# A performer attention and token/channel mixer on one Trainium2 core: the order of all jobs, their buffer slots and the choice of eviction engines are made anew

## The chip, the cores and the metric

The kernel runs on one NeuronCore of one Trainium2 chip. TensorE (PE) multiplies matrices into PSUM banks; VectorE (DVE), ScalarE (ACT) and GpSimd (POOL) do the elementwise work and move results out of PSUM; SyncE (SP), ACT and POOL also issue DMAs. Each engine works through its own list of instructions in order and waits on semaphores for the others. The metric is device microseconds for one execution of the whole kernel, as the median of several runs.

## What is computed

The reference, cut to what matters: random-feature attention (a "performer") for 8 batches, 8 heads, 576 positions and head size 64 with 128 features, and behind it a mixer over tokens (256 hidden) and over channels (512 wide, 1536 hidden).

```python
def phi(x):
    proj = np.einsum('bhsd,md->bhsm', x, omega)
    sq = np.sum(x * x, axis=-1, keepdims=True) / 2.0
    h = proj - sq
    h = h - np.max(h, axis=-1, keepdims=True)
    return np.exp(h) / np.sqrt(m)
q_p, k_p = (phi(q_s), phi(k_s))          # q, k times 1 / 64 ** 0.25
kv = np.einsum('bhsm,bhsd->bhmd', k_p, v)
z = np.sum(k_p, axis=2)
num = np.einsum('bhsm,bhmd->bhsd', q_p, kv)
den = np.einsum('bhsm,bhm->bhs', q_p, z)[..., None] + 1e-06
x = (num / den)                          # heads side by side: (8, 576, 512)
h = np.maximum(xt @ w_tok1, 0.0) @ w_tok2   # xt: x with tokens last
u = x + h.transpose(0, 2, 1)
out = u + np.maximum(u @ w_ch1, 0.0) @ w_ch2
```

## The kernel before

Matmuls take f16 operands, and PSUM holds f32 in eight banks of 128 x 512. Work is cut into some 1200 numbered jobs: a matmul job fills one bank (four matmuls of 512 columns for a channel job `c1`), an eviction job empties it.

For each batch b from 0 to 7 there are these stages. k and q are loaded and turned so that the head dimension lies on the partitions (`kT`, `qT`): batches 0 and 1 on TensorE (`first_rows`, `rows`, evicted by `first_out` and `rows_out`), the later ones by a cast to a scratch in DRAM and a transposing DMA that SP issues (`back`, L380). Each batch has 576 positions; the last 64 of all heads go together as a tail (`kt`, `qt` and what belongs to them). `kp` and `qp` multiply by omega, and ACT evicts them with the exponential (`kp_exp`, `qp_exp`, helper line L515). DVE takes a maximum for k (`km`, L681), v is scaled by it (`vs_`, L689, by the helper `tt` at L295), `kv` sums over the positions, and its eviction is `kv_out` (kvsb). `num` multiplies by qp, and DVE divides on eviction (`num_out`, L744 and L745). The token mixer is `t1` with a relu, `t2` and `uadd`; `ut_dma` (L799) is SP's transposing DMA that makes `uT`, the channel mixer's input. Batch 0 makes it on TensorE instead (`ut_`, evicted by `ut_out`).

The channel mixer runs over nine blocks c: 512 positions of each batch, and c8 with the 64-position tails of all batches. `c1` (L967, for the first two jobs of c0 split into L973 and L975) has twelve jobs of 128 hidden rows by 512 positions, each with a `relu` to `r` (L290 on ACT, L292 on DVE). Block 0 multiplies by the second weight wc2 in the usual way (`c2`, L1001). The others use one level of Strassen's scheme (`channel_out_fast`): eight sums of halves of r for each block (L877, by `tt`), seven products (L917), and reads that add them up in the output tile (`read`, L906), then stores. The differences of wc2's quarters that it needs are four `T` jobs on DVE (L448), which need both halves of wc2 (L440).

The order is not found at build time. Three tables hold it. ORDER lists the job numbers; `Planner.run` (L137) goes through it and issues each job on its engine, so each engine's list of instructions is ORDER cut to its jobs. A negative number n is a warm-up: a matmul of zeros into bank -1-n (L1039), of which there are 23. SLOT gives each buffer of a ring (banks, kT, qT, uT, r and others) its place in the ring, in the order in which they are first taken. MOVED overrides the engine of a job by its number:

```python
def engine(self, usual):
    return MOVED.get(len(self.jobs), usual)
```

The helper of the elementwise sums looks at the name of the engine in this way, while evictions have a form for ACT and one for DVE:

```python
def tt(eng, **kw):
    (nc.gpsimd if eng == "POOL" else nc.vector).tensor_tensor(**kw)
```

In the old order SP issues a first k load (job 4, L385), omega (job 2, L395) and a second k load (6); ACT issues the other two k loads (3 and 5). Job 7 is the k tail's load, 0 the identity matrix, both on POOL. Job 39 is the transpose of omega (L452), 41 and 44 are `first_rows` (L470), 47, 48, 67 and 68 belong to the k tail of batch 0. POOL issues the loads of v, q, the weights and the casts, in one queue.

Of the kernel before, what the change touches and what calls it, by code (L numbers as in the profile page):

```python
# [81 lines left out]
]  # L82
SLOT = (
    "0001203450670100531642027046313724005203716031213170242506371243501030126450300623741115037622415010"
    "3157143302010163207240531170360711422336140014632220751302761220105427113005401216030201704522131743"
    "5632010231741610520432015370243105072320714330625120712006304015123156124230220105611334112101502001"
# [985 lines left out]
```

## Time and profile before

| | us |
|---|---|
| median of 3 runs | 282.96 (282.94 to 283.96) |
| span of the profiled execution, first to last instruction | 281.1 |
| TensorE busy in it | 270.3 |
| VectorE busy | 222.4 |
| ScalarE busy | 138.6 |
| GpSimd busy | 92.0 |

The profiled execution is known by its span; the runs' times contain what lies around it, so the median is 1.9 us above this span. In the profile "PE" is a matmul, "PEld" a load of weights. L967 is line 967 of the kernel as listed above. In rows of waits, "A <- B" means that A waited for B. In the changed kernel all lines behind the tables have a number lower by 18.

### The profile page before, as it was taken

Reading aid. Unit: us, or ns where it says so; the run is one execution under the profiler, and the core shown is the slowest. Engines: PE = TensorE matmul, PEld = TensorE weight load, DVE = VectorE, ACT = ScalarE, POOL = GpSimd, SP = SyncE. Lnnn points to the kernel's source line nnn. Section 1 sums busy time; section 2 is a strip of 40 time slices with the busy share of each in tenths; the row PEclk is TensorE's granted clock in tenths of the full one; section 3 lists DMA queues with packets and bytes.
Section 4 is the critical chain, followed back from the end, with each engine's and each line's share of the span. In section 5 each row is a group of like instructions: output and inputs, shape, how many; then the busy total and the mean of one; then the engine's idle time right before and its main releaser. Section 6 shows DMA issues by size and latency. Waiting matters only on the chain.

```text
span 281.1 us, 6278 instructions
## 1 busy us (share of the span) xinstructions
PE 270.3 (96%) x2526; PEld 167.6 (60%) x2526; DVE 222.4 (79%) x462; ACT 138.6 (49%) x288; POOL 92.0 (33%) x116
## 2 busy tenths in 40 slices
PE   6899999999999999999999999999999999999993
PEld 2547546443657755665667647755676467446782
DVE  2589828499999899996997999977995893565992
ACT  1498994049676418743758445734753510031200
POOL 8574994007510872048008710510033000000001
PEclk9999999999999999999999999999999999999999
DMA  6999999999998999997979993960151304030125
GB/s 161 194 189 161 157 169 213 178 191 202 179 218 184 148 172 186 181 198 104 212 178 185 241 135 101 161 156 2 76 97 59 111 0 96 0 149 2 75 90 135
DMA packets 80524, 39.66 MB, mean 141 GB/s; under 512 B 63984, under 2 KB 76016, under 8 KB 80304
## 3 DMA queue, kind: packets, MB, share of 16 engines
q0 software_dynamic: 31744, 17.74, 44.1%
q1 hardware_dynamic: 46832, 15.77, 29.1%
q10 hardware_dynamic: 1920, 5.77, 5.4%
q8 instruction: 19, 0.31, 0.4%
q14 instruction: 9, 0.07, 0.1%
HBM read 35.95 MB, written 16.52 MB: 187 GB/s over the span
## 4 chain that ended last, share of the span: by engine, by line
PE 89%; DVE 3%; DMA 2%; ACT 2%; issue 0%; SPq 0%; DVEq 0%
PE bank L967 32%; PE bank L917 26%; PE bank L791 5%; PE bank L778 5%; PE bank L1001 4%; PE bank L735 3%; PE bank L657 3%; PE bank L702 3%; DMA wc<-in_k_dram 2%; PE bank L669 2%; ACT kp L515 1%; PE bank L845 1%; PE bank L817 1%; PE bank L737 1%; PE bank L771 1%; DVE T L448 1%
## 5 line engine op out<-in xcount | busy, mean ns | idle before, releaser
L967 PE MATMUL bank<-uT,wc 128*128 128x512 f16 x376 | 89.6, 379 | 0.5 <-DVE r L292 0.4
L290 ACT ACTIVATE r<-bank 128x512 f16<-128x512 f32 (+1 forms) x86 | 47.7, 601 | 82.7 <-PE bank L967 61.5
L295 POOL TENSOR_TENSOR vs<-v,vs 128x512 f16<-128x512 f16 x32 | 34.2, 1072 | 94.4 <-DVE vs L683 51.3
L967 PEld LDWEIGHTS <-wc 128*128 128x128 f16 x424 | 38.8, 98 | 38.8 <-issue 1.6
L917 PEld LDWEIGHTS <-r 128*128 128x128 f16 x384 | 36.8, 98 | 8.2 <-issue 1.1
L515 ACT ACTIVATE kp<-bank 128x512 f16<-128x512 f32 x64 | 36.7, 618 | 8.9 <-PE bank L657 7.1
L515 ACT ACTIVATE qp<-bank 128x512 f16<-128x512 f32 x64 | 36.7, 614 | 8.8 <-PE bank L669 5.8
L681 DVE TENSOR_REDUCE km<-kp 128x8 f16<-128x1024 f16 x32 | 38.7, 1208 | 1.2 <-ACT kp L515 1.1
L292 DVE TENSOR_SCALAR r<-bank 128x512 f16<-128x512 f32 (+1 forms) x40 | 26.3, 670 | 15.7 <-PE bank L967 11.3
L745 DVE TENSOR_TENSOR x<-bank,rc 128x320 f16<-128x320 f32 x62 | 30.5, 492 | 2.1
L917 PEld LDWEIGHTS <-S 128*128 128x128 f16 x288 | 28.1, 98 | 5.8 <-issue 0.3
L906 DVE TENSOR_TENSOR o<-u,bank 128x512 f32<-128x512 f16 x28 | 19.0, 679 | 6.2 <-PE bank L917 5.8
L917 PE MATMUL bank<-T,r 128*128 128x256 f16 x192 | 23.8, 273 | 0.0
L917 PE MATMUL bank<-wc,r 128*128 128x256 f16 x192 | 23.6, 273 | 0.0
L917 PE MATMUL bank<-T,S 128*128 128x256 f16 x192 | 23.4, 273 | 0.0
L946 POOL DMA_DIRECT2D out_dram<-o x2 | 1.3, 645 | 61.2 <-issue 61.2
L906 DVE TENSOR_TENSOR o<-o,bank 128x512 f32<-128x512 f32 (+1 forms) x27 | 16.6, 617 | 2.5 <-PE bank L917 1.8
L735 PEld LDWEIGHTS <-qp 128*128 128x128 f16 x256 | 13.5, 98 | 8.1 <-DVE kvsb L286 0.7
L794 DVE TENSOR_TENSOR u<-x,bank 128x512 f16<-128x512 f16 x28 | 17.6, 680 | 0.0
L735 PE MATMUL bank<-kvsb,qp 128*128 128x65 f16 x256 | 15.0, 193 | 0.5 <-DVE kvsb L286 0.5
L791 PE MATMUL bank<-r,w 128*128 128x512 f16 x56 | 14.1, 381 | 0.0
L744 DVE RECIPROCAL rc<-bank 128x5 f32<-128x5 f32 x62 | 11.4, 184 | 2.9 <-PE bank L737 2.2
(119 smaller groups left out, 379.0 us busy)
## 6 DMA issues: line engine op xcount, KB each, us to landing
out_dram<-o ACTq DMA_DIRECT2D x9, 512.0 KB, 2.7
q<-in_q_dram POOLq DMA_DIRECT2D x6, 576.0 KB, 9.7
wc<-in_moe_w_ch_dram POOLq DMA_DIRECT2D x4, 768.0 KB, 9.0
k<-in_k_dram POOLq DMA_DIRECT2D x6, 512.0 KB, 7.8
v<-in_v_dram POOLq DMA_DIRECT2D x6, 512.0 KB, 9.9
out_dram<-o SPq DMA_DIRECT2D x5, 512.0 KB, 3.9
r<-in_q_dram POOLq DMA_DIRECT2D x4, 288.0 KB, 7.5
v<-in_v_dram POOLq DMA_DIRECT2D x4, 256.0 KB, 8.1
```

The costliest lines, as they stand in the source:

```text
L290: nc.scalar.activation(out=out, in_=in_, func=AF.Relu)
L292: nc.vector.tensor_relu(out=out, in_=in_)
L295: (nc.gpsimd if eng == "POOL" else nc.vector).tensor_tensor(**kw)
L515: nc.scalar.activation(out=out, in_=in_, func=AF.Exp, bias=0.0, scale=1.0)
L681: nc.vector.reduce_max(out=mx, in_=kpv, axis=AX.X)
L735: nc.tensor.matmul(ps[:, k, j * 65 : (j + 1) * 65], st, s[:, i, 0 : D + 1], start=True, stop=True)
L745: nc.vector.tensor_tensor(out=t_x[place("x", b)][:, :, (2 * hp + hs[0]) * D : (2 * hp + hs[0] + n) * D].rearrange("p j (i d) -> p i j d", ...
L791: nc.tensor.matmul(ps, w2_of(tb, j), r1[:, tb, :], start=(tb == 0), stop=(tb == NT - 1))
L794: nc.vector.tensor_tensor(out=t_u[place("u", b)][:, j, :], in0=t_x[place("x", b)][:, j, :], in1=bank(n), op=ALU.add)
L906: nc.vector.tensor_tensor(out=o, in0=a, in1=ps, op=ALU.add)
L917: nc.tensor.matmul(ps[:, j * DH : (j + 1) * DH], a[:, cb, j * P : (j + 1) * P], w[:, cb, :], start=(bank_of(b, j0) not in held and j == j0 ...
L967: nc.tensor.matmul(ps, wc1[:, db, cb * P : (cb + 1) * P], moving(db), start=(db == 0), stop=(db == ND - 1))
```

## The change

All three tables are replaced; everything below them is the same. The diff, cut to its core:

```diff
 ORDER = [
-    4, 3, 0, 2, 5, 7, 1, 6, 16, 14, 10, 15, 9, 8, 12, 38, 11, -1, -2, -3, -4, -5, -6, -7, -8, 39, 41, 13, 44,
-    42, 21, 40, 47, 45, 48, 76, 22, 46, 77, 67, 43, 68, -4, -6, 120, 18, 105, 78, 107, 82, -3, 49, 71, 106, 122,
-    -5, 90, 51, 111, 91, -4, -4, 52, 17, 70, 19, 121, 50, 53, 83, 54, 92, 126, -5, -5, -5, -1, -1, -6, -3, -1,
-    72, 69, 30, 108, 79, 110, 84, 112, 80, 96, 55, 81, 127, 113, 74, 73, 123, 109, 75, 28, 128, 124, 85, 114,
-    86, 57, 56, 97, 115, 88, 129, 87, 125, -8, 61, 20, 93, 89, 98, 94, 23, 116, 130, 134, 95, 131, 31, 99, 117,
...
+3, 7, 2, -1, 5, 4, 0, -2, 6, 10, 1, 9, 8, 12, 38, 39, 11, 40, 16, 13, 47, 48, 21, 67, -3, 68, 22, 41, 70, -3, 42, 43, -6, 14, 69, 76, 90, 18, 78, -2,
+91, 17, -3, 44, 77, 71, -6, 92, 49, 82, -6, 45, 50, 105, 52, 96, 107, 19, 79, 106, -6, 83, 46, -6, -2, 53, 81, 120, 30, 84, 51, 121, 108, 122, 54, 97,
+-1, 109, 93, 111, -6, 94, 72, 28, 74, 55, 110, 98, 85, 112, 95, 57, -8, -2, 73, 123, 126, 56, 219, 75, 80, 61, 20, 99, -3, 221, 63, -5, 88, 125, 127,
+100, -5, 89, 220, 86, 113, 101, 23, 87, 247, 114, 102, 103, -1, 31, 104, 134, 124, 115, 62, 24, 117, 128, 249, 118, 116, 64, 25, 135, -4, 129, 119,
+65, 205, 460, 130, 138, 131, 248, 132, 142, 66, 207, 58, 196, 139, 133, 236, 29, 60, 140, 143, 206, 59, 146, 33, 141, 253, 202, 238, 197, 144, 199,
...
+331, 161, 213, 327, 167, 256, 229, 214, 259, 332, 257, 230, 231, 241, 171, 164, 242, 152, 258, 215, 217, 165, 191, 34, 243, 260, 176, 216, 245, 181,
+244, 232, 186, 246, 182, 218, -8, 35, 261, -8, 264, 36, 262, 329, 265, 183, 263, 177, 184, 268, 328, 266, 269, 272, 267, 270, 178, 273, 271, 187, 179,
...
 ]
 SLOT = (
-    "0001203450670100531642027046313724005203716031213170242506371243501030126450300623741115037622415010"
...
+    "01010100340320541102600152431270053104716020340560417031361152065020430205006217105233076430123006145037007216470265210413670057622436061720"
...
 )
 MOVED = {
-    42: "DVE", 43: "ACT", 45: "ACT", 48: "DVE", 51: "ACT", 53: "ACT", 56: "ACT", 60: "ACT", 62: "ACT", 65:
-    "ACT", 75: "DVE", 129: "ACT", 137: "DVE", 139: "DVE", 141: "DVE", 145: "ACT", 147: "DVE", 163: "ACT", 169:
-    "DVE", 171: "ACT", 175: "DVE", 179: "ACT", 190: "ACT", 194: "ACT", 228: "ACT", 242: "DVE", 256: "DVE", 265:
-    "DVE", 278: "DVE", 280: "DVE", 286: "DVE", 300: "DVE", 324: "ACT", 399: "DVE", 426: "DVE", 428: "DVE", 432:
-    "DVE", 434: "DVE", 484: "DVE", 498: "DVE", 552: "DVE", 556: "DVE", 562: "DVE", 593: "ACT", 594: "ACT", 634:
-    "DVE", 662: "DVE", 690: "DVE", 692: "DVE", 700: "DVE", 702: "DVE", 727: "ACT", 768: "DVE", 796: "DVE", 822:
-    "DVE", 828: "DVE", 830: "DVE", 836: "DVE", 838: "DVE", 863: "ACT", 904: "DVE", 970: "DVE", 997: "ACT", 998:
-    "ACT", 1024: "DVE", 1052: "DVE", 1088: "DVE", 1092: "DVE", 1094: "DVE", 1096: "DVE", 1098: "DVE", 1102:
-    "DVE", 1104: "DVE", 1108: "DVE", 1133: "ACT", 1134: "ACT", 1140: "DVE", 1148: "DVE", 1150: "DVE", 1152:
-    "DVE", 1160: "DVE", 1200: "SP", 1205: "ACT", 1206: "SP", 1207: "ACT", 1208: "SP",
+42: "DVE", 43: "ACT", 45: "ACT", 46: "ACT", 50: "ACT", 56: "ACT", 60: "ACT", 114: "ACT", 129: "ACT", 143: "DVE", 147: "DVE", 163: "ACT", 175: "DVE",
+179: "ACT", 184: "ACT", 189: "ACT", 190: "ACT", 194: "ACT", 195: "ACT", 226: "DVE", 240: "DVE", 256: "DVE", 286: "DVE", 292: "DVE", 296: "DVE", 300:
+"DVE", 301: "ACT", 302: "ACT", 304: "ACT", 306: "ACT", 307: "ACT", 308: "ACT", 350: "DVE", 364: "DVE", 378: "DVE", 390: "DVE", 401: "DVE", 416: "DVE",
+422: "DVE", 424: "DVE", 428: "DVE", 436: "ACT", 440: "ACT", 441: "ACT", 526: "DVE", 568: "DVE", 570: "DVE", 571: "ACT", 573: "ACT", 574: "ACT", 576:
+"ACT", 577: "ACT", 578: "ACT", 620: "DVE", 648: "DVE", 671: "DVE", 692: "DVE", 696: "DVE", 702: "DVE", 704: "DVE", 706: "ACT", 707: "ACT", 708: "ACT",
+710: "ACT", 711: "ACT", 768: "DVE", 782: "DVE", 794: "DVE", 805: "DVE", 830: "DVE", 832: "DVE", 834: "DVE", 836: "DVE", 841: "ACT", 842: "ACT", 844:
+"ACT", 846: "ACT", 847: "ACT", 863: "ACT", 864: "ACT", 890: "DVE", 902: "DVE", 904: "DVE", 930: "DVE", 939: "DVE", 952: "DVE", 964: "DVE", 972: "DVE",
+977: "ACT", 978: "ACT", 980: "ACT", 981: "ACT", 982: "ACT", 998: "ACT", 1024: "DVE", 1038: "DVE", 1052: "DVE", 1066: "DVE", 1075: "DVE", 1088: "DVE",
+1090: "DVE", 1092: "DVE", 1096: "DVE", 1100: "DVE", 1104: "DVE", 1110: "DVE", 1111: "ACT", 1113: "ACT", 1114: "ACT", 1115: "ACT", 1116: "ACT", 1117:
+"ACT", 1134: "ACT", 1140: "DVE", 1144: "DVE", 1150: "DVE", 1154: "DVE", 1158: "DVE", 1163: "ACT", 1164: "ACT", 1166: "ACT", 1168: "ACT", 1169: "ACT",
+1170: "ACT", 1202: "ACT", 1205: "ACT", 1207: "ACT", 1208: "SP",
 }
```

What it changes, as read off the two orders:

- SP issues omega (2) ahead of its two k loads (4, 6). On POOL the load of the k tail (7) comes ahead of the identity matrix (0).
- Two warm-ups, in place of eight, stand ahead of the transpose of omega (39); the others lie between the first matmul jobs. The k tail of batch 0 (47, 48, 67, 68) comes before `first_rows` (41, 44).
- POOL's loads and casts keep their order. On SP some transposing DMAs and stores change places.
- The number of jobs of each kind stays. Six `vs_` products go from POOL to DVE; one copy `qt_dup` goes from DVE to POOL; DVE has 18 `kv_out` in place of 14, 42 channel and token relus in place of 40, 9 of 12 `rows_out` in place of 6; ACT has all four `out_copy` in place of two. Of the last stores ACT issues 7, SP 4 and POOL 1, where it was 4, 6 and 2.
- 42 of the 64 sums of Strassen's scheme are named "ACT" in MOVED.
- The first `T` (34) stands ahead of `num_out` jobs of batch 1 (260, 216, 244, 232, 246, 218). The `kt` matmuls of batch 4 stand some 20 us of TensorE work earlier.
- kT of batches 2 to 5 all take place 0 of their ring, those of 6 and 7 place 1; uT of all batches takes place 1. Banks are taken again at other distances.

More of the change, by code (lines that the diff above doesn't have):

```diff
@@ L22 @@
 ORDER = [
[59 rows of a table removed]
[42 rows of a table added]
 ]
 SLOT = (
-    "0001203450670100531642027046313724005203716031213170242506371243501030126450300623741115037622415010"
-    "3157143302010163207240531170360711422336140014632220751302761220105427113005401216030201704522131743"
-    "5632010231741610520432015370243105072320714330625120712006304015123156124230220105611334112101502001"
-    "1163320402165140211610176412517304000612037524002145223000117023104325137202120117305042100576141135"
-    "2740507154076110042751603114022705011041315732121403000112045010725110200405061403012301765403706427"
@@ L89 @@
-    "5643015206241073100625101246023220116534201330523111135160224716051246514725364700113516422103135174"
-    "1625317524300060120373642501100433627516043075122761076423700560420017305611117230017341570146002140"
-    "73521450047113602"
+    "01010100340320541102600152431270053104716020340560417031361152065020430205006217105233076430123006145037007216470265210413670057622436061720"
+    "10217061023450367235110020051716701522430123531704603214016201713715624011213064052173543104713226012702342011635004115012703116373160321053"
@@ L92 @@
+    "00312020061022012041141060701106270214133562047130201350362053206714313114070261702415310126716105113041510020123356012714201532411071260733"
+    "40734205370611400004131114105614261150172301702526420103215020506710417112616514302173236412460412700511510140301032741112063010422011322115"
+    "61502403717410023027170510651724336205303561070211406243206112107210142070406103622362411017472476167401470160162101411207270520257600702601"
+    "52110555006502415"
 )
 MOVED = {
-    42: "DVE", 43: "ACT", 45: "ACT", 48: "DVE", 51: "ACT", 53: "ACT", 56: "ACT", 60: "ACT", 62: "ACT", 65:
```

89 rows, old and new, of the table ORDER are left out of this document.

## The prediction

> **What bounds the kernel now.** I read the page from the top: the busy shares, the slices, and the chain that ended last.
>
> ```profile
> PE 270.3 (96%) x2526; PEld 167.6 (60%) x2526; DVE 222.4 (79%) x462; ACT 138.6 (49%) x288; POOL 92.0 (33%) x116
> PE   6899999999999999999999999999999999999993
> ACT  1498994049676418743758445734753510031200
> PE 89%; DVE 3%; DMA 2%; ACT 2%; issue 0%; SPq 0%; DVEq 0%
> ```
>
> TensorE is 96% busy and is 89% of the chain. The change keeps all 2526 matmuls, so it can only give back time in which TensorE has nothing to do. The windows show where that is, and ACT beside it: it is 49% busy over the run but 80 to 90% busy in slices 3 to 6 of 7 us each, 14 to 42 us.
>
> ```profile
> 0.00:10.00 10.00, 5.93 (x41) 3.08 (x42) 2.37 (x14) 1.28 (x1) 6.60 (x15) 1.00 0.87 168
> 10.00:20.00 10.00, 9.65 (x140) 5.00 (x137) 8.47 (x14) 8.84 (x20) 7.84 (x10) 1.00 1.22 205
> 20.00:33.50 13.50, 12.65 (x224) 9.23 (x224) 11.85 (x30) 12.59 (x35) 9.47 (x13) 1.00 1.04 149
> 33.50:276.10 242.60, 241.89 (x2128) 150.30 (x2127) 199.33 (x405) 115.90 (x234) 68.08 (x80) 1.00 0.76 137
> 276.10:281.10 5.00, 0.13 (x2) 0.00 (x0) 0.42 (x1) 0.00 (x0) 0.00 (x0) 0.89 0.54 146
> ```
>
> The columns after the length are PE, PEld, DVE, ACT, POOL (count in brackets), granted clock, DMA share and GB/s. From 33.5 us on TensorE is busy 241.89 of 242.60 us. The view of TensorE's waits over that stretch names only these two:
>
> ```profile
> PE bank L967 <- DVE r L292: 0.4, 1, 0.4
> PE bank L771 <- DVE x L745: 0.3, 1, 0.3
> ```
>
> Before 33.5 us the busy share misleads, since a recorded matmul is much longer than its turn. The chain has four L967 matmuls of 512 columns in 0.86 us, 0.215 each; at such paces the 405 matmuls before 33.5 us hold 16.0 us of real work and 4.9 us of warm-ups (23 x 0.215). Some 17.5 us without real work lie there. The chain of waits says on what:
>
> ```profile
> 0.74 0.68 SPq L385
> 1.48 0.57 SPq L395
> 2.09 6.97 DMA wc<-in_k_dram
> 9.10 1.12 PE bank L470 x13
> 13.32 1.57 ACT kp L515 x3
> 20.62 0.83 DVE qpt L631
> ...
> 32.80 0.70 DVE uT L286
> 33.54 1.02 PE bank L967 x4
> 41.07 0.86 PE bank L967 x4
> ```
>
> First the k loads (omega queued behind one on SP), then ACT's exponentials at 0.52 us each, then vector work up to the transposed mixer input uT, which frees the first channel matmul L967 at 33.54 us. Everything later is nearly gapless: what the change can win is that date, and the end.
>
> **The start.** SP now issues omega first: 0.74 us instead of 1.48. The POOL queue issues the k tails ahead of the identity matrix. TensorE does the k tails before the k rows, so ACT's first eviction no longer waits for the last k load.
>
> ```profile
> 6.40 0.29 PE L452 MATMUL bank<-ident,S 128*128 128x128 f16 x1 [1.61 <-DVE S L450]
> 10.16 0.59 ACT L286 CAST kT<-bank 128x512 f16<-128x512 f32 x1 [6.51 <-PE bank L470]
> L515 ACT ACTIVATE kp<-bank 128x512 f16<-128x512 f32 x13 | 7.8, 631 | 1.1 <-PE bank L657 1.0
> L515 ACT ACTIVATE qp<-bank 128x512 f16<-128x512 f32 x10 | 5.9, 643 | 0.5 <-PE bank L669 0.5
> ```
>
> (The last two rows are the groups of ACT from 10 to 33.5 us.) With omega 0.74 us sooner its transpose L452 runs at about 5.7 and ACT can start at about 7.0 in place of 10.16. The k load that SP moves back behind omega loses 0.74 us itself, but its rows are used later. Before the first L967 the old order holds 20.6 us of ACT work (each kind at its spacing when back to back, 0.52 for a kp): 10.16 + 20.6 + 1.6 idle = 32.4, and then DVE's km and uT end at 33.5. The new order has 22.35: more kp, qp, first_out and one more uT, less rows_out. Never idle, ACT ends at 7.0 + 22.35 = 29.35; with 1.0 of idle, 30.35; with uT evicted by ACT last and DVE's km no longer ahead of it the first L967 comes between 30.4 and 32.5 (if half of it fails). I take 31.0: 2.5 us earlier, and 0.3 us more real work is done by then (16.3 against 16.0).
>
> **What meets the earlier start.** The POOL order of the loads is kept, and they do not all come 2.5 us earlier.
>
> ```profile
> L440 POOL DMA_DIRECT2D wc<-in_moe_w_ch_dram x2: 846/862/877, 31.9 to 34.4; - x2
> DMA to landing us min/median/max: 7.4/10.3/12.7
> 47.68 4.10 PE bank L1001 x19
> 53.71 2.71 SPq L380 DMA_TRANSPOSE kT<-k  x1
> 60.55 1.85 SPq L799 DMA_TRANSPOSE uT<-u  x1
> 65.42 1.73 DVE T L448
> 67.92 1.89 PE bank L967 x8
> ```
>
> The last half of wc2 is issued at 34.4 and lands 12.7 later, at 47.1; L1001, its first reader, starts at 47.68. Ahead of it the queue ran at 149 GB/s from 20 to 33.5 us against 205 from 10 to 20. Were all that made up, (205-149)/205 x 13.5 = 3.7 us would come back; two dips, at 20 to 24 and 28 to 32 us, look like POOL issuing late, so I take 2.4. wc2 then lands at 44.7, and L1001, which comes at 28.9 us of real work in place of 29.2, can start at 44.8. The loads of k for batch 2 follow in the same queue, then kT's transpose (53.7) and uT's (60.55): about 2.4 earlier too. L967 of batch 1 starts near 63.05 instead of 64.95, but at 0.45 us less work done: 1.5 us of the gain is left at 65 us. Bounds: 0 (the queue saturated) and 2.5.
>
> **Engines and order afterwards.** Six vs products leave POOL for DVE, one dup copy (0.83 above) goes from DVE to POOL, and a few evictions change engine.
>
> ```profile
> L295 POOL TENSOR_TENSOR vs<-v,vs 128x512 f16<-128x512 f16 x32 | 34.2, 1072 | 94.4 <-DVE vs L683 51.3
> L295 DVE TENSOR_TENSOR S<-r 128x768 f16<-128x768 f16 x16 | 8.8, 551 | 0.6 <-ACT r L290 0.4
> ```
>
> No vs on DVE is in the trace; between the larger sum there, 0.551, and POOL's 1.072 I take 0.55: 3.3 us more on DVE over 200 us in which it idles 43, so nothing on the path (up to 6.4 us of DVE time, covered the same way; without the idle time it would delay evictions, rival 4). The T subtractions L448 that held L967 at 67.92 go ahead of num_outs as soon as wc2 is there, and the wait at L771 has another order: I take both waits, 0.4 + 0.3 = 0.7, as gone (bounds 0 and 0.7).
>
> The new order uses the PSUM banks more tightly. Counted over both orders after the start, a bank is taken again within 1.2 us of TensorE work after the job that filled it in 19 places before and 73 now, in 36 of these at about one job of four matmuls, 0.86.
>
> ```profile
> L967 PE MATMUL bank<-uT,wc 128*128 128x512 f16 x376 | 89.6, 379 | 0.5 <-DVE r L292 0.4
> L290 ACT ACTIVATE r<-bank 128x512 f16<-128x512 f32 (+1 forms) x86 | 47.7, 601 | 82.7 <-PE bank L967 61.5
> L292 DVE TENSOR_SCALAR r<-bank 128x512 f16<-128x512 f32 (+1 forms) x40 | 26.3, 670 | 15.7 <-PE bank L967 11.3
> ```
>
> A last matmul of 0.379 and an eviction of 0.601 or 0.670 free the bank 0.77 to 0.83 us after that matmul's turn of 0.215: inside 0.86, by 0.03 to 0.09 us, if the evicting engine is free. Where it isn't, TensorE stands. The small gaps of the old order at its 19 places come to about 0.8 us, an estimate from starts of neighbouring matmuls; scaled by 73/19, 2.3 us more. Bounds 0 and 2.3; I take 0.4, since in most of the 54 new places the engine has nothing queued by the order.
>
> The transposed loads have less room. The kt matmuls of batch 4 move some 20 us of work earlier and keep their kT buffer in one slot with the batch before; uT of batches 3 and 7 has 7.4 us between the last t2 matmul and the first L967, where it had 9.3 and 10.9.
>
> ```profile
> DMA to landing us min/median/max: 5.7/6.8/8.9
> ```
>
> This is kT's transpose from issue to landing: at its maximum 2.1 us over its median. I take nothing, as by my count the dates are just met; one late by half that, 1 us, at each of the three places costs 3 us.
>
> **The end.** The tail's stores lie differently: ACT issues seven, SP four, POOL one.
>
> ```profile
> 274.74 3.33 ACTq L946 DMA_DIRECT2D out_dram<-o  x4
> ```
>
> ACT's last four issues took 3.33 us; with one more at that rate behind the last read the end is up to 0.8 later; I take 0.2, since the last two issues are split over both queues as before.
>
> **The sum.** Start 1.5 + waits 0.7 - banks 0.4 - tail 0.2 = 1.6 us saved. The span of 281.1 becomes 279.5. The median of the runs lies 1.9 over the span (282.96 - 281.1), so the time is 281.4 us.
>
> **A rule against it.** The new order has 2 warm-ups ahead of the omega transpose, the old one 8:
>
> ```profile
> 1.19 3.60 PE L1039 MATMUL bank<-S 128*128 128x512 f16 x8 [1.19 <-DVE S L1036]
> 11.28 1.04 PE L1039 MATMUL bank<-S 128*128 128x512 f16 x2
> ```
>
> Eight in 3.60 us are 0.45 each, twice the 0.215 of later: TensorE starts at half pace although the granted clock reads 1.00, and two at 11.28 still take 0.52 each. The Trainium skill, "TensorE: Matmul & The Clock Gate", "Part 1: The HAM clock gate", says that the array starts at half clock and comes to full only after a busy window of about 3.4 us. The trace agrees with the first half; the eight did not hold the pace through the pauses behind them. By that rule the new order stays at half pace for longer, and it is a rival below.
>
> **The rivals.**
> 1. The whole start gain survives: POOL, no longer waiting, fills both dips and more, and wc2 lands as early as TensorE gets there. For it: DMA ran at 205 GB/s right before. Against it: each dip is only some 2 us deep, and more than 205 GB/s is in none of the windows. 1.0 to 1.3 more than in the sum: 280.2 us.
> 2. The queue holds all of it: wc2 lands at 47.1 as before, and L1001 and all after stand where they stood. 281.4 + 1.5 = 282.9.
> 3. Fewer warm-ups: if the real matmuls before 15 us, about 5 us of work, run at half pace, 5 us are added, but ACT's evictions bound that stretch, so 0 to 1.5 reach the first L967. With 1.0: 282.4.
> 4. Slower: banks. In all 54 new places evictions come 0.1 us later than planned (an ACT relu behind another eviction, a DVE one behind a 1.2 us km). The place is every L967 stretch from 65 us on; the price 54 x 0.1 = 5.4 in place of 0.4: 286.4. It decides where the last matmul's start to the end of the eviction exceeds 0.86 + 0.215 = 1.08 us, 0.1 over what the two rows add up to. For it: the margin is 0.03 to 0.09. Against it: the old order's 19 places cost about 0.04 each.
> 5. Slower: late transposes. kT of batch 4 and uT of batches 3 and 7 miss by about 1 us each: 284.4. For it: latencies spread by 2 us. Against it: a delay once taken moves all that follows, and the next has more room.
> 6. The change does not do what it says: it names ACT for 42 of the 64 Strassen sums (L295), but the helper for them knows only POOL and VectorE, so they stay on DVE. If the order counts on a free DVE there, the last sums of each of 8 blocks come some 0.6 late: 281.4 + 4.8 = 286.2. Against it: the sums stand in the order as close to the next DVE job as the ones named for DVE do.
>
> **How the numbers follow.** The forecast has 0.36, rival 1 0.15, 2 0.10, 3 0.05, 4 0.20, 5 0.10, 6 0.04. By its bounds the forecast's own case goes from 280.3 to 282.3. About 0.5%, 1.4 us, is what a measurement can tell here: faster means below 281.55, slower above 284.37. The forecast gives 0.27 to faster and 0.09 to no change; with rival 1 faster is 0.42. No change is 0.09 + 0.10 + 0.04 = 0.23. Rivals 4, 5, 6 and a rest of 3 make 0.35 slower. The range leaves out the best tenth (start gain 3 and both waits, 279.3) and the worst (above 286.8, half a us over rival 4): 279.3 to 286.8.
>
> **What would show it.** Right: L452 near 5.7 us, ACT's first eviction near 7, the first L967 near 31, L1001 near 44.8, L967 of batch 1 near 63, no wait at T, and the last 240 us gapless. Wrong: L1001 still near 47.6 (rival 2), warm-ups and kp matmuls at 0.4 past 12 us with a first L967 past 32 (3), many short gaps before L967 with ACT or DVE evictions as releasers (4), waits on kT or uT (5), S matmuls that wait for L295 (6).

## The result, and the profile after

The changed kernel takes 296.45 us (median) against 283.37 for the kernel before on the same chip: ratio 1.0441, interval 1.0381 to 1.0501. Timed again on another chip it is 1.0412 (1.0363 to 1.0461), 297.1 against 285.37. It is slower by about 12 us, where 1.6 us less was forecast. (One of its four first executions, the one profiled first, took 304.78 us; its extra 8 us are a single wait, told at the end. The profile below is of a later execution, e17, without that wait and with a span of 295.3 us. It lies 14.2 us above the trace of before, but the two come from different chips; timed side by side on the chip of e17 the difference is 11.7 us.)

The changed kernel: busy times, the slices of TensorE, and the windows that were shown of before.

```profile
PE 273.9 (93%) x2526; PEld 167.5 (57%) x2526; DVE 229.3 (78%) x471; ACT 138.4 (47%) x284; POOL 86.1 (29%) x110
...
PE   2999999999799799999969999999999999999991
```

```profile
0.00:10.00 10.00, 4.75 (x34) 1.93 (x36) 2.63 (x12) 3.27 (x7) 6.58 (x15) 1.00 0.89 170
10.00:20.00 10.00, 9.53 (x147) 4.96 (x145) 7.44 (x14) 9.35 (x20) 8.13 (x11) 1.00 1.22 205
20.00:33.50 13.50, 13.33 (x227) 9.46 (x226) 11.07 (x27) 12.61 (x34) 11.46 (x15) 1.00 1.20 175
33.50:276.10 242.60, 233.95 (x2021) 140.77 (x2020) 197.01 (x396) 113.13 (x225) 59.24 (x69) 1.00 0.75 130
```

In this execution the start is where it was: taken as one window, the first 33.5 us hold 400 matmuls, as against 398 (the sums over shorter windows, 408 and 405, count a matmul on an edge twice). The loss lies behind it. In the same stretch of 242.6 us TensorE does 2021 matmuls instead of 2128, and its busy time falls from 241.89 to 233.95. The other engines are busy for less of the stretch too, since less of the work passes in it: DVE 197.01 (199.33 before), ACT 113.13 (115.90), POOL 59.24 (68.08). Over the whole execution DVE has more to do, 229.3 us instead of 222.4, but that is 78% of a longer span. So TensorE waits on engines that are not full. These are the rows of 0.5 us and more behind the start in the view of its waits, where before only two rows stood in all:

```profile
PE bank L949 <- DVE o L888: 1.6, 1, 1.6
PE bank L651 <- DMA qT<-q: 1.5, 1, 1.5
PE bank L684 <- DVE u L776: 1.4, 1, 1.4
PE bank L773 <- DVE ut L833: 1.1, 1, 1.1
PE bank L899 <- DVE o L888: 0.9, 2, 0.6
PE bank L639 <- DVE r L274: 0.6, 1, 0.6
PE bank L773 <- DVE r L274: 0.5, 2, 0.3
PE bank L773 <- DVE u L776: 0.5, 1, 0.5
```

Seven of the eight wait for VectorE: for reads (`o`), adds of the token mixer (`u`, `ut`) and relus (`r`). With the smaller rows TensorE's waits for VectorE behind the start are 7.5 us, against 0.7 before. From the start of the first channel matmul to the start of the last matmul it takes 255.5 us, against 242.4: 13.1 us more. A count of work says in what pieces: it takes off each matmul's usual spacing from the next one's start, and what is left over is a gap. The gaps behind the first channel job are 17.0 us against 3.9 before by this count: some 31 of them are over 0.12 us and make 14.5 us (before 6, 1.6 us). The gaps below 0.12 us are 2.45 us in all against 2.29.

The largest shows how one comes about. TensorE and then DVE of the changed kernel around 97 us (start, duration, engine and line, and in brackets what ended an idle time):

```profile
96.96 0.41 PE L684 MATMUL bank<-vs,kp 128*128 128x65 f16 x8
97.20 0.22 PE L691 MATMUL bank<-vbd,kpt 128*128 128x130 f16 x1
99.03 1.24 PE L949 MATMUL bank<-uT,wc 128*128 128x512 f16 x5 [1.61 <-DVE o L888]
```

```profile
95.17 1.22 DVE L663 TENSOR_REDUCE km<-kp 128x8 f16<-128x1024 f16 x1
96.42 0.21 DVE L665 RECIPROCAL vs<-km 128x8 f16<-128x8 f16 x1
96.54 1.83 DVE L277 TENSOR_TENSOR S<-r,S 128x768 f16<-128x768 f16 x2
98.30 0.68 DVE L888 TENSOR_TENSOR o<-u,bank 128x512 f32<-128x512 f16 x1
```

L949 needs the bank that the read L888 empties. DVE gets to that read at 98.30, after two Strassen sums that take 1.83 us. Both are the last sums of block 1, and both are named "ACT" in the new table. The first takes 0.51 us, but the second 1.41, and it runs beside a product on POOL:

```profile
96.71 1.25 POOL L277 TENSOR_TENSOR vs<-v,vs 128x512 f16<-128x512 f16 x1 [0.39 <-DVE vs L665]
```

In the kernel before all 64 sums take 0.55 to 0.56 us, and none of them runs beside a POOL addition or product. Here four take 1.14 to 1.41. So of the 1.83 us that hold up the read, some 0.85 are that one of the sums is slow there.

### The profile page after: what moved, and what is told of

It reads as the page before. It is cut to its first block, busy times and chain, and to the rows that moved or that the text cites. A ratio compares the mean times of both kernels' runs of the same rounds, so it can differ in the third digit from the quotient of the medians.

```text
span 302.9 us, 6263 instructions
## 1 busy us (share of the span) xinstructions
PE 275.6 (91%) x2526; PEld 167.7 (55%) x2526; DVE 228.1 (75%) x471; ACT 138.2 (46%) x284; POOL 86.1 (28%) x110
## 4 chain that ended last, share of the span: by engine, by line
PE 62%; DVE 19%; DMA 10%; ACT 4%; issue 3%; SPq 1%; DVEq 0%; POOLq 0%
PE bank L949 19%; PE bank L899 19%; DMA kT<-k 8%; DVE S L277 4%; PE bank L760 4%; DVE x L727 3%; PE bank L773 3%; PE bank L983 3%; DVE r L274 3%; PE bank L639 2%; DVE o L888 2%; PE bank L651 2%; DVE km L663 2%; DMA r<-in_k_dram 2%; PE bank L684 2%
## 5 line engine op out<-in xcount | busy, mean ns | idle before, releaser
L949 PE MATMUL bank<-uT,wc 128*128 128x512 f16 x376 | 90.1, 379 | 1.6 <-DVE o L888 1.4
L949 PEld LDWEIGHTS <-wc 128*128 128x128 f16 x424 | 38.8, 98 | 42.7 <-issue 4.1
L277 POOL TENSOR_TENSOR vs<-v,vs 128x512 f16<-128x512 f16 x26 | 28.2, 1089 | 82.5 <-DVE vs L665 65.8
L274 DVE TENSOR_SCALAR r<-bank 128x512 f16<-128x512 f32 (+1 forms) x42 | 27.7, 667 | 21.9 <-PE bank L949 11.9
L497 ACT ACTIVATE qp<-bank 128x512 f16<-128x512 f32 x64 | 37.4, 615 | 4.9 <-PE bank L651 4.8
L888 DVE TENSOR_TENSOR o<-u,bank 128x512 f32<-128x512 f16 x28 | 19.1, 682 | 6.8 <-PE bank L899 6.7
L277 POOL TENSOR_TENSOR vbd<-vt,vbd 128x512 f16<-128x512 f16 x6 | 6.3, 1050 | 55.8 <-DVE vbd L576 28.4
L717 PEld LDWEIGHTS <-qp 128*128 128x128 f16 x256 | 14.2, 98 | 7.6 <-DVE kvsb L268 0.3
L888 DVE TENSOR_TENSOR o<-o,bank 128x512 f32<-128x512 f32 (+1 forms) x27 | 16.4, 621 | 2.5 <-PE bank L899 1.5
L717 PE MATMUL bank<-kvsb,qp 128*128 128x65 f16 x256 | 16.2, 193 | 0.0
L773 PE MATMUL bank<-r,w 128*128 128x512 f16 x56 | 14.8, 381 | 1.1 <-DVE u L776 0.5
## 6 DMA issues: line engine op xcount, KB each, us to landing
wc<-in_moe_w_ch_dram POOLq DMA_DIRECT2D x4, 768.0 KB, 10.9
```

The source lines that it names most:

```text
L274: nc.vector.tensor_relu(out=out, in_=in_)
L497: nc.scalar.activation(out=out, in_=in_, func=AF.Exp, bias=0.0, scale=1.0)
L717: nc.tensor.matmul(ps[:, k, j * 65 : (j + 1) * 65], st, s[:, i, 0 : D + 1], start=True, stop=True)
L773: nc.tensor.matmul(ps, w2_of(tb, j), r1[:, tb, :], start=(tb == 0), stop=(tb == NT - 1))
L888: nc.vector.tensor_tensor(out=o, in0=a, in1=ps, op=ALU.add)
L949: nc.tensor.matmul(ps, wc1[:, db, cb * P : (cb + 1) * P], moving(db), start=(db == 0), stop=(db == ND - 1))
```

## The experiments

**1. The same kernel again (e1), and one transposing load moved (e3).** The profile taken first had TensorE wait 7.8 us for the transposing load of k for batch 6 (job 869), which the new order issues ahead of two stores (458, 457).

> The changed kernel as it is, for a second profile; the first had the granted clock at 0.50 to 0.87 around 150 us and a TensorE wait of 7.8 us on the transposing load of k for batch 6. Theory A (that one load is the main loss): the wait is there again, 5 to 8 us, in a span near 294.5. Theory B (many small waits: tighter banks and fewer ring places): the wait at batch 6 is under 2 us, and 10 us or more are lost in pieces below 1.5 us.

```diff
 ORDER = [
...
-    455, 648, 452, 869, 446,
+    455, 648, 452, 446,
...
-    561, 548, 457, 664, 635,
+    561, 548, 457, 869, 664, 635,
```

> The changed kernel with the transposing load of k for batch 6 put back behind the two stores of block 2 in SP's queue, as before. If three transposing loads in a row beside v and q loads make it slow (A): it takes about 4 us instead of 17 to issue, TensorE waits for it at most 4 us, and the time falls by 4 to 8 us from a run with that wait. If the loss is many small waits (B): the time stays near 296.

e1: span 295.9 and 297.68 us, with no wait at batch 6; e3: span 295.4 and 297.77 us. Theory A falls for the loss as a rule: the 12 us are there without that wait. What e3 does in an execution that has it was not seen.

**2. omega ahead of k alone (e2).**

```diff
-    4, 3, 0, 2, 5, 7, 1, 6,
+    2, 4, 3, 0, 5, 7, 1, 6,
```

> The kernel before with one edit: SP issues omega ahead of its first k load. If the start hangs on omega: the first L967 up to 0.7 us earlier, 0.3 to 0.7 us less in all. If on the last k load or on ACT: within 0.3 us of before. Neither theory of the loss expects it slower by more than 0.5 us.

Ratio 0.9989 (0.9969 to 1.0009): nothing that can be told from no change. By the count of work the first channel job came 0.15 us earlier.

**3. Rings in turn (e4).** The new tables use place 0 of kT four times running, and place 1 of uT seven times. Here kT, qT, u, r1 and uT take their three places in turn, which changes 25 digits of SLOT:

```diff
 SLOT = (
-    "0101010034032054110260015243127005310471602034056041703136115206502043020500621710523307...
+    "0101010034032054110260015243127005310471602034056141703136115206502043020500621711523307...
```

> The changed kernel with the rings of kT, qT, u, r1 and uT used in turn over their three places, order and engines as in the changed kernel. If places taken again too soon hold up loads and writes (B, the rings): 3 to 8 us faster than the changed kernel, waits on kT, qT and u gone. If the rings do not matter: within 1 us of the changed kernel.

Ratio 1.0444 (1.0385 to 1.0502), and 12.5 us lost behind the start, as in e1. The places of these five rings do not matter.

**4. The sums that are named for ACT (e5, e6, and timed again as e18, e19 beside e17).** The labels change no instruction, but an order made in the belief that ACT does this work would give DVE's time to others. e5 lets ACT do as much as a sum would: a copy.

```diff
     def tt(eng, **kw):
+        if eng == "ACT":
+            return nc.scalar.copy(out=kw["out"], in_=kw["in0"])
         (nc.gpsimd if eng == "POOL" else nc.vector).tensor_tensor(**kw)
```

> The changed kernel, in which the 42 Strassen sums that are named for ACT are ACT copies of their first operand, so 42 additions are left out. If the order counts on ACT for them, and DVE has them on top (the rival of the prediction): TensorE's waits on DVE reads and uadds near 98, 150 and 153 us vanish, and the time falls by 4 to 9 us. If DVE's load there is not the cause: it falls by less than 2 us, or rises as ACT gets the work.

e6 leaves them on DVE, but short:

```diff
-                    tt(e_sum, out=o[:, part], in0=a[:, part], in1=b[:, part], op=op)
+                    w = slice(0, 32 if e_sum == "ACT" and c > 1 else 2 * P)
+                    tt(e_sum, out=o[:, part, w], in0=a[:, part, w], in1=b[:, part, w], op=op)
```

> The changed kernel, in which those of the 42 sums that belong to blocks 2 to 8 (36) stay on DVE but only add the first 32 of 256 columns of each piece; the rest is left out. DVE loses some 36 x 0.4 = 14 us of work and ACT gets none. If DVE's load is the cause: 4 to 9 us faster, as with the copies or more. If not: within 2 us of the changed kernel.

The first times were few and far apart (e5 287.98 and 292.24 us, ratio 1.0232, interval 1.0053 to 1.0412; e6 289.81 and 299.97 us), so both were timed again beside the changed kernel.

> The changed kernel again, timed beside the next two on one chip. By all theories 296 to 298.

> The 42 sums named for ACT as copies on ACT again (additions left out), timed in more rounds. If DVE's extra load is the larger part: 7 to 9 us below the changed kernel, so 288 to 290, and 4 to 6 over before.

> 36 of the sums cut on DVE again, timed in more rounds. If DVE's extra load is the larger part: 6 to 9 us below the changed kernel, 288 to 291. If the first times (289.8 and 300.0) meant that it does not help in general: above 293.

On that chip: changed 1.0412 (above), copies 1.0140 (1.0052 to 1.0228), cut 1.0156 (1.0092 to 1.0220). The cut takes 0.0256 x 285.37 = 7.3 us off the loss, the copies 7.8 by these ratios. The cut is the firm one: its four executions took 288.79 to 291.25 us, against 297.01 to 298.48 for the changed kernel. Those of the copies took 288.23, 291.08, 295.65 and 301.39; the ratio is of the two shortest, and the median of all four, 293.36, misses what was expected. The one of 295.65 left a trace: there TensorE waits 5.1 us for transposing loads of q and k, and 0.6 us for VectorE.

The traces say the same with less scatter. TensorE's waits for VectorE behind the start, 7.5 us in the changed kernel (7.3 in e1), are 0.4 with copies (e5) and 2.8 with cut sums (e6, e19), 1.6 of this the wait of block 1. From the first channel matmul to the last matmul it takes 255.5 us in the changed kernel (254.7 in e1), 247.3 in e5, 248.1 in e6 and 248.4 in e19, where before has 242.4. The rows behind the start in e5:

```profile
PE bank L686 <- ACT qp L499: 0.9, 1, 0.9
PE bank L653 <- DMA qT<-q: 0.5, 1, 0.5
PE bank L775 <- ACT qp L499: 0.5, 1, 0.5
PE bank L775 <- ACT qpt L499: 0.2, 1, 0.2
PE bank L641 <- DVE x L729: 0.2, 1, 0.2
PE bank L951 <- DVE ut L835: 0.2, 1, 0.2
```

The windows from 33.5 to 276.1 us, first of the kernel with cut sums (e19), then of the one with copies (e5):

```profile
33.50:276.10 242.60, 238.24 (x2074) 145.28 (x2073) 190.25 (x406) 114.18 (x228) 59.18 (x70) 1.00 0.75 132
```

```profile
33.50:276.10 242.60, 239.66 (x2089) 146.68 (x2086) 183.20 (x368) 143.44 (x267) 58.93 (x69) 1.00 0.74 134
```

The place of the 1.61 us wait, in the kernel with copies (its lines are numbered two higher, TensorE first, then DVE, then ACT):

```profile
95.91 0.41 PE L686 MATMUL bank<-vs,kp 128*128 128x65 f16 x8
96.15 0.22 PE L693 MATMUL bank<-vbd,kpt 128*128 128x130 f16 x1
96.21 2.54 PE L951 MATMUL bank<-uT,wc 128*128 128x512 f16 x11
```

```profile
95.38 0.21 DVE L667 RECIPROCAL vs<-km 128x8 f16<-128x8 f16 x1
95.50 0.64 DVE L890 TENSOR_TENSOR o<-u,bank 128x512 f32<-128x512 f16 x1
```

```profile
94.55 1.57 ACT L278 COPY S<-r 128x768 f16<-128x768 f16 x2
```

The two sums' worth of work is on ACT at 94.55, in a place that the order leaves free there. DVE's read follows the reciprocal at once (95.50), and eleven channel matmuls run on with no wait. In the kernel with cut sums this very wait remains, as it should: its two sums belong to block 1, which is not cut there.

**5. The control on the old order (e13).** The same 36 sums, cut in the same way, in the kernel before; for this MOVED names the 42 sums "ACT" there too, which by the helper alone changes nothing.

```diff
-                    tt(e_sum, out=o[:, part], in0=a[:, part], in1=b[:, part], op=op)
+                    w = slice(0, 32 if e_sum == "ACT" and c > 1 else 2 * P)
+                    tt(e_sum, out=o[:, part, w], in0=a[:, part, w], in1=b[:, part, w], op=op)
```

> Control: the kernel before with the same 36 sums of blocks 2 to 8 cut to 32 of 256 columns on DVE; the rest of them is left out. If DVE's load is a loss by itself: several us faster than before. If only an order made without it loses: within 1 us of before, since the old order has room for them.

Ratio 1.0000 (0.9974 to 1.0026).

```profile
33.50:276.10 242.60, 241.75 (x2128) 150.36 (x2128) 188.45 (x406) 116.01 (x234) 68.22 (x80) 1.00 0.76 137
```

DVE has 199.33 - 188.45 = 10.9 us less to do, and TensorE does the same 2128 matmuls. The load is no loss in itself; it is one under an order without room for it. Whether other work of the same size, cut on DVE, would gain as much under the new order was not tested.

**6. The same sums elsewhere: on POOL (e9), or late on DVE (e12).**

```diff
 MOVED = {
-... 301: "ACT", 302: "ACT", 304: "ACT", ... 1170: "ACT",
+... 301: "POOL", 302: "POOL", 304: "POOL", ... 1170: "POOL",
```

> The changed kernel with the 42 sums that are named for ACT named for POOL, which the helper knows; nothing left out. If DVE's load is the cause of the loss: as with the copies on ACT, 4 to 8 us faster than the changed kernel, less what the slower POOL (estimated 1.55 us for 768 columns, from 1.05 for 512) delays a product. If not: no faster than 1 us.

Ratio 1.0915 (1.0839 to 1.0991): worse by 13 us than the changed kernel. The instructions of e9 that write S (min/median/max in ns, first and last start) say why:

```profile
L280 POOL TENSOR_TENSOR S<-S,r x12: 1622/1638/1946, 87.2 to 295.4; 128x768 f16<-128x768 f16 x12
L280 DVE TENSOR_TENSOR S<-S,r x4: 561/2212/3772, 85.5 to 292.5; 128x768 f16<-128x768 f16 x4
```

A sum takes 1.64 us on POOL, and four sums form a chain; TensorE's products then wait for POOL (6.0 us in four waits). The row of DVE is four of the 22 sums left there; of these 22, the nine with no POOL addition or product beside them take 0.55 to 0.56 us, and the 13 others have a median of 1.40. So e9 says nothing against the cause, and isn't a repair.

e12 only moves 34 of the sums in the list, each later; the first of them, 301, goes 19 places:

```diff
 ORDER = [
...
-    597, 368, 301, 351, 353,
+    597, 368, 351, 353,
...
+    400, 276, 301,
...
```

> The changed kernel with 34 of the 42 sums moved back in DVE's list alone, to 1.3 us of TensorE work ahead of the product that reads them (0.6 us more for each sum that follows in its chain). Same work, engines and places. If the loss is the order (sums ahead of evictions that TensorE waits for): 3 to 7 us faster than the changed kernel. If it is DVE's load as such: within 2 us of it.

Ratio 1.0438 (1.0364 to 1.0511): nothing. The waits changed their names: two of TensorE's waits were now for the sums themselves (1.3 us in all), others for reads and adds as before. TensorE's waits for VectorE are 7.3 us, as in e1. Of the two outcomes expected this is the one of the load: shifting one kind of job within a list that has no room there moved the waits and didn't take them away.

**7. The two halves of the order (e7, e8).** Old tables up to the first channel job and new ones behind it (e7), and the other way about (e8); here the seam in ORDER, e7 first.

```diff
-    250, 200, 235, 160, 251, 249,
+    250, 200, 235, 249, 248, 236, 253,
...
-    233, 149, 222, 153, 224, 234,
+    233, 149, 222, 15, 225, 223, 224,
```

> The order, places and engines of the kernel before up to the first c1 job, and from there those of the changed kernel. If the start costs 2 us and the rest 10 to 12: about 2 us faster than the changed kernel, 294. If the losses behind the start come from it: near 284.

> The order, places and engines of the changed kernel up to the first c1 job, and from there those of the kernel before. If the start costs 2 us by itself: about 286. If the old rest absorbs it, its gaps being free there: 284. If the new start is a gain that the rest loses: below 282.

New start and old rest: 1.0050 (1.0006 to 1.0093), 1.4 us over before; nearly all of the 12 us goes with the new rest. Old start and new rest is 1.0629 (1.0598 to 1.0660), 5 us worse than the changed kernel itself: by the count of work it loses some 5 us around the seam, where neither order was made for the other, so it adds nothing on the start.

**8. The start taken apart (e10, e15).**

```diff
-    3, 7, 2, -1, 5, 4, 0,
+    3, 7, -1, 5, 4, 2, 0,
```

> The changed kernel with SP's first k load put back ahead of omega. If omega's place costs the start, by delaying that k load from 4.2 to 6 to 7.5 us: the first k rows are turned earlier and the start is 0.5 to 1.5 us earlier than in the changed kernel. If the k tail being first on TensorE costs it (a wait of 3 to 4 us on its load): no change, since that wait stays.

Ratio 1.0461 (1.0403 to 1.0519), start within what the changed kernel shows from run to run. Here omega landed at 6.05 us, behind the k tail's load (5.75), and the first kp was evicted only at 12.24. e15 also sets the k rows first:

```diff
-    47, 48, 21, 67, -3, 68, 22, 41, 70, -3, 42, 43, -6, 14, 69, 76, 90, 18,
+    41, 42, 43, -3, -3, -6, 76, 90, 47, 48, 21, 67, 68, 22, 70, 14, 69, 18,
```

> The changed kernel with the old sequence of the start: k ahead of omega on SP, and the k rows of heads 0 to 3 with their first two kp jobs ahead of the k tail on TensorE. If the k tail at the head is what costs the start: TensorE's wait of 3 to 5 us on the tail's load goes, the first kp comes about 2 us earlier, and the first L949 1 to 2 us earlier than in the changed kernel. If ACT's work bounds the start anyway: within 0.5 us. The loss behind the start stays near 12 us by all theories.

Ratio 1.0537 (1.0497 to 1.0577), with the start 2 us later than in e1: its TensorE waited 4.7 us for omega, and ACT stood with the k tail's exponentials between the rows. It puts a wait for omega in place of the one for the tail's load, so it doesn't settle whether the k tail at the head holds the start. The traces do (next section).

**9. A version to beat both (e16).** In the kernel before, T jobs 35 and 36 behind the relu 278.

```diff
-... 389, ... 35, ... 36, ... 278,
+... 389, ... 278, 35, 36,
```

> A try for a version that beats both: the kernel before with two of its T subtractions moved behind the one relu that they held up on DVE (a TensorE wait of 0.4 to 0.6 us at 67 us). If the wait was a real one: 0.4 to 0.6 us less, ratio 0.998. If another wait follows at once: no difference.

Ratio 1.0005 (0.9976 to 1.0033). The count of work shows the 0.6 us won at 67 us, and a new loss of 1.1 by 80 us. No version that beats the kernel before was found.

## Why the prediction was wrong, step by step

**What bounds the kernel** was read rightly: TensorE, with the start as the only stretch that has time to give. That also meant that the rest could only lose, by 12 us as it turned out, and the prediction gave that too little weight.

**The start** failed as a term of the sum. The prediction had ACT begin near 7.0, idle 1.0 us, and the first channel job at 31.0. The first matmul of the k tail on TensorE and then ACT of the changed kernel, in the execution above:

```profile
6.10 0.39 PE L487 MATMUL bank<-ident,r 64*128 64x64 f16 x4 [2.76 <-DMA r<-in_k_dram]
```

```profile
6.53 0.37 ACT L268 COPY ktt<-bank 128x256 f16<-128x256 f16 x1 [1.56 <-PE bank L487]
8.25 0.63 ACT L546 ACTIVATE kpt<-bank,kt_nb 128x128 f16<-128x128 f32 x2 [1.35 <-DVE kt_nb L540]
10.49 2.06 ACT L497 ACTIVATE kp<-bank 128x512 f16<-128x512 f32 x4 [0.37 <-PE bank L639]
```

Its first channel job on TensorE:

```profile
33.62 0.82 PE L955 MATMUL bank<-uT,wc 128*128 128x512 f16 x3
```

ACT begins at 6.53 as foreseen, but the first kp is evicted only at 10.49. From 6.53 to 10 it is busy 3.27 - 1.28 (a table load) = 1.99 us of 3.47, and from 10 to 33.5 it is busy 9.35 + 12.61 = 21.96 of 23.5: it idles 1.48 + 1.54 = 3.0 us and is busy 24.0, where 1.0 and 22.35 were put in. That is 3.6 us, more than the 2.6 by which the first channel job (33.62, here L955) missed 31.0. And the date isn't steady: by the count of work the start lay between 0.2 us ahead of before and 2.2 behind it in executions of the same tables. What moves it is the load of the k tail, which the new order puts first on TensorE. The same two places in e1, whose first channel job came at 35.97:

```profile
7.33 0.39 PE L487 MATMUL bank<-ident,r 64*128 64x64 f16 x4 [4.00 <-DMA r<-in_k_dram]
11.73 1.57 ACT L497 ACTIVATE kp<-bank 128x512 f16<-128x512 f32 x3 [0.37 <-PE bank L639]
```

In the 12 traces that have the new start as it is, this load lands between 6.06 and 8.18 us, and the first kp is evicted 4.43 to 4.44 us after it lands, whatever the date. So the new order takes ACT's first eviction off the last k load, as predicted, and hangs the first kp on the tail's load instead; at best it came at 10.49, where it was at 10.80 before. The gain "1.5 of it survives" was nothing to begin with: the last half of wc2 did land 1.7 us earlier in e17 (45.4), but its first reader came at 47.0 instead of the 44.8 foretold, and the channel mixer of batch 1 began at 65.1, as before (65.0).

**Omega and the queue.** Issued first, omega landed at 2.6 us in place of 5.8, earlier than forecast; the k load behind it on SP landed at 5.4 to 7.6 in place of 4.3. e2 puts the two together at nothing.

**The two waits taken as gone** (0.7 us): the one at T is gone, the other is gone in e17 and 0.2 to 0.3 us in two other traces. Both are outdone by the list above.

**The tail**, 0.2 in the sum: from the start of the last matmul to the end it takes 5.1 us before, 5.3 in the execution profiled first and in e1, and 6.2 in e17.

**The banks**, rival 4, with 0.4 us in the sum, are borne out as small by the count of work, though no run puts the old distances back: 54 more places of tight reuse, and gaps below 0.12 us of 2.45 against 2.29. The bank that TensorE waited for at 99 us was late by 1.6 because the evicting engine was busy elsewhere, not because the reuse distance was short.

**Rival 6 was the one that decided**, with a chance of 0.04 and a time of 286.2. The sum has no term for these sums at all, and the step that put them at nothing is the "against" of rival 6: the sums stand in the order as close to the next DVE job as the ones named for DVE do. A distance to the next job says nothing of whether that engine has time then. The same fault is in the step on the engines, which puts more work on DVE at nothing because DVE idles 43 us (of 242.6) in all: idle time in the sum does not lie where an order needs it. e5, e19 and e13 together show the mechanism: the sums that are named "ACT" cost 7 to 8 us on DVE under the new order (the 36 of blocks 2 to 8 alone 7.3), and those 36 nothing under the old. Its price was too small as well. It had one late sum of 0.6 us for each of 8 blocks, 4.8 us, but the sums delay whatever stands behind them on DVE: reads, adds and relus. So the sign named for it, S matmuls that wait for the sums, is not in the traces of the changed kernel; the waits carry the names of the jobs behind them.

**What is left** after the sums, 1.4 to 1.6% or 4 to 4.5 us, wasn't taken apart. In the kernel with cut sums the gaps behind the start are 9.9 us against 3.9 before. Its uncut block 1 still has the gap of 1.78 us; qT of batch 3 comes 1.4 late, which is the kind of rival 5 (at another batch than named there), and the others are 0.3 to 0.6. The six vs products now on DVE are part of what is open, since no run puts them back on POOL.

**The warm-ups**, rival 3: no run here tells a loss by them at the start from the one by the load.

## What to carry to other kernels

A table that names an engine is a belief of whoever made the order; read the helper that executes it, and take a name that it doesn't know as a fault in the order, priced by what stands behind that work on the engine that really does it. An even load says little when an order is fixed: the same 36 sums were free under one order and cost 7 us under another, and leaving the work out of both kernels told that apart, where moving it about (e9, e12) told nothing. A kernel whose bound engine is 96% busy has few us to win and many to lose by a new order.

## What the hardware showed that was not expected

Transposing loads can get slow beside others. In the execution profiled first, SP issued transposing loads at 122.58, 125.48 and 127.93 us while POOL had just issued loads of v and q. First the last of them in SP's timeline, then TensorE's wait, then windows of 4 us (the columns as above):

```profile
127.93 17.39 SPq L362 DMA_TRANSPOSE kT<-k  x1
```

```profile
PE bank L534 <- DMA kT<-k: 7.8, 1, 7.8
```

```profile
134.00:138.00 4.00, 4.00 (x52) 2.37 (x51) 2.78 (x10) 3.23 (x8) 0.00 (x0) 1.00 1.45 53
138.00:142.00 4.00, 4.00 (x24) 1.81 (x22) 3.19 (x9) 3.73 (x8) 1.75 (x2) 1.00 1.21 54
...
146.00:150.00 4.00, 0.00 (x0) 0.00 (x0) 0.00 (x0) 0.00 (x0) 3.33 (x4) 0.78 1.10 162
150.00:154.00 4.00, 2.49 (x10) 0.92 (x11) 0.00 (x0) 0.62 (x2) 0.00 (x0) 0.50 1.08 284
```

The issue took 17.39 us where the other kT and qT take at most 3.8, and the DMA engines were fully busy (the share is over 1) at 53 and 54 GB/s, a quarter of the 217 and 218 that they moved between 122 and 130 us. Why, and why only in some executions, stays open. In and behind the wait the granted clock reads 0.78 and 0.50, and eight matmuls of 512 columns behind it take 3.48 us, some 0.43 each where 0.215 is usual: an estimate of 1.7 us on top of the wait. This agrees with the Trainium skill, "TensorE: Matmul & The Clock Gate", "Part 1: The HAM clock gate", by which the array falls back to half clock after an idle window of about 3.4 us.

A DVE addition or product of two f16 tiles is slower beside one on POOL: in e9 the 13 sums on DVE that ran beside one took a median of 1.40 us and up to 3.77, where a sum alone takes 0.55 to 0.56. POOL's vs products hardly change, with a mean of 1.09 us in the changed kernel against 1.07. The six vs products moved to DVE took 0.77 us there in the mean (five some 0.68, the one beside POOL 1.20), more than the 0.55 that the prediction put in; what that costs on the path was not tested.
